# Gated linear attention and a gated feed-forward layer in one kernel: unit 0 through both ACT tables at once, loads reordered, decay and transposes moved

## Chip, cores and metric

The kernel runs on one core of a Trainium2 chip. The metric is the device time of one execution in microseconds (us). Engines: PE (matmul), PEld (its weight loads), DVE (VectorE), ACT (ScalarE), POOL (GpSimd, which here mostly issues the casting DMAs) and SP (SyncE, which issues the plain DMAs). "The trace" is the record of one profiled execution; its span is about 2 us shorter than the time.

## The reference, cut to what matters

```python
# attention: batch 4, 8 heads, 768 steps, head size 48; a decaying complex state per head
a_re, a_im = scaled so that |a| <= 0.999
for t in range(768):
    S_re, S_im = (a * S)_re + k[t] v[t]^T, (a * S)_im
    y[t] = q[t] @ S_re
# feed-forward on x = y as [3072 tokens, 384]
out = x + sigmoid(x @ w_res) * ((gelu(x @ w_gate) * (x @ w_val)) @ w_out)
```

The product of the decays over time is turned into cumulative sums of log-magnitude and angle. So each block of 256 steps needs Ln and Exp of `a` (one ACT table, a set of functions that ACT loads before it uses them, 1.28 us in these traces), then arctan and sin (another table); the feed-forward needs Gelu (a third).

## The kernel before

A group `g` is 256 steps of one batch (12 groups), a unit `u` is two groups (6 units). The program is software-pipelined. `phase_x(u)` does *gate math*: Ln/Exp for unit u+2 and u+1, arctan for u+2, sin for u+1, half of the attention of unit u, and the output matmuls (`op`) of unit u-1. `phase_y(u)` does the *gates*: `gp`, `vp`, `rp` of unit u, and the other half of an attention. A scheduler turns this program order into each engine's own order; in the timelines below an engine does not pass an instruction that waits. `E` and `Ei` are the exps of the cumulated log-magnitude and of its negative; `Q` and `K` are q and k multiplied by these and by the sines and cosines, made by DVE and then transposed by PE. "First Q" below is PE's first transpose of Q.

```python
    def p1_steps(g):
        ...  # lm = Ln(a_re); th = Exp(-lm) * a_im; s = Ln(1 + th^2); lm = min(lm + s/2, LNMAX)
    def decay(g):            # factor by which the state decays between groups: one [1,384] row of
                             # each of three tiles, turned to [96, 8] by way of DRAM
        md = dr.tile([3, DM], FP, tag="md", name="md")
        nc.gpsimd.dma_start(out=md[0:1, :], in_=T["E", g - 1][127:128, DM:W])
        nc.gpsimd.dma_start(out=md[1:2, :], in_=T["Ei", g][0:1, 0:DM])
        nc.gpsimd.dma_start(out=md[2:3, :], in_=T["lm", g][0:1, 0:DM])
        m3 = mp.tile([128, 3, H], FP, tag="m3", name="m3")
        for u in range(2):
            nc.gpsimd.dma_start(out=m3[u * D:(u + 1) * D]..., in_=md.rearrange("r (h d) -> d (r h)", h=H))
    def decay2(g):
        act(out=m3[0:DD, 2], in_=m3[0:DD, 2], func=AF.Exp)     # ACT waits for the DRAM round trip
        ...                                                    # M = product of the three, on DVE
    def xt_step(u, jj):      # x of one 128-token chunk, transposed for the feed-forward
        tpx = psT.tile([128, DM], BF, tag="tp", padded_shape=[128, 1024], name="tpx")
        ...
    def att_steps(u, half):
        steps = []
        for g in gs(u)[half:half + 1]:
            for c in range(C):
                steps += attention(g, c)
                steps.append(call(xt_step, u, half * C + c))
        return steps
    def phase_x(u):
        ...
        weave((0.0, 0.12, front), (0.05, 0.55, p1), (0.12, 0.45, exs), (0.46, 0.46, dec), (0.25, 0.65, cst),
              (0.69, 0.69, dec2), (0.7, 0.95, table_trig), (0.0, 0.8, att_steps(u, 1)), (0.1, 1.0, ops))
    ...
    for g in gs(0):
        load_a(g); load_q(g)               # (cut to one line each)
    for g in gs(1): load_a(g)
    for g in gs(1): load_q(g)
    for u in range(-2, NU + 1):            # two empty pipeline phases before unit 0's gates
        phase_x(u)
        if u == -2:
            load_w()                       # all weights, whole rows, no wait
        phase_y(u)
        ...
```

`weave` places lists of steps at fractions of a phase. `a`, `q`, `k` are loaded by SP; `v` and the weights are cast to bf16 while loading, by DMAs that POOL issues (the software queue).

Of the kernel before, what the change touches and what calls it, by code (L numbers as in the profile page):

```python
# [9 lines left out]
FP = mybir.dt.float32  # L10
BF = mybir.dt.bfloat16
AF = mybir.ActivationFunctionType
# [16 lines left out]
def kernel(  # L29
# [55 lines left out]
    wr = singles.tile([128, KD, DM], BF, name="wr")  # L85


    lda = ctx.enter_context(tc.tile_pool(name="lda", bufs=3))
    ldq = ctx.enter_context(tc.tile_pool(name="ldq", bufs=3))
    ldv = ctx.enter_context(tc.tile_pool(name="ldv", bufs=6))  # L90
    pA = ctx.enter_context(tc.tile_pool(name="pA", bufs=4))
    pS = ctx.enter_context(tc.tile_pool(name="pS", bufs=2))
    pE = ctx.enter_context(tc.tile_pool(name="pE", bufs=2))
    pQ = ctx.enter_context(tc.tile_pool(name="pQ", bufs=2))
# [24 lines left out]
    def act(**kw):  # L119
        tab(nc.scalar.activation(**kw))  # L120
# [22 lines left out]
            nc.gpsimd.dma_start(out=t[:, c], in_=rows(v, g, c))  # L143
        T["v", g] = t

    def load_w():
        for i in range(KD):
            nc.gpsimd.dma_start(out=wg[:, i, :], in_=moe_w_gate[i * 128:(i + 1) * 128, :])
            nc.gpsimd.dma_start(out=wv[:, i, :], in_=moe_w_val[i * 128:(i + 1) * 128, :])
        nc.gpsimd.dma_start(out=wr, in_=moe_w_res.rearrange("(i p) m -> p i m", p=128))  # L150
        for i in range(0, KF, 4):
            nc.gpsimd.dma_start(out=wo[:, i:i + 4, :],
                                in_=moe_w_out[i * 128:(i + 4) * 128, :].rearrange("(i p) m -> p i m", p=128))

    def flat(t):
        return t.rearrange("p c h d -> p (c h d)")


    def p1_steps(g):
        def s0():  # L160
            T["lm", g] = pA.tile([128, W], FP, tag="lm", name="lm")
            act(out=T["lm", g], in_=flat(T["ar", g]), func=AF.Ln)

        def s1():
            T["th", g] = pA.tile([128, W], FP, tag="th", name="th")
            act(out=T["th", g], in_=T["lm", g], func=AF.Exp, scale=-1.0)
            nc.vector.tensor_tensor(out=T["th", g], in0=T["th", g], in1=flat(T["ai", g]), op=OP.mult)  # L167

        def s2():
            T["s", g] = pS.tile([128, W], FP, tag="s", name="s")  # L170
            act(out=T["s", g], in_=T["th", g], func=AF.Square)

        def s3():
            act(out=T["s", g], in_=T["s", g], func=AF.Ln, bias=1.0)
            lm = T["lm", g]
            nc.vector.scalar_tensor_tensor(out=lm, in0=T["s", g], scalar=0.5, in1=lm, op0=OP.mult, op1=OP.add)
            nc.vector.tensor_scalar(out=lm, in0=lm, scalar1=LNMAX, scalar2=None, op0=OP.min)  # L177

        return [s0, s1, s2, s3]
# [5 lines left out]
    def cs_l(g, c):  # L185
# [9 lines left out]
            act(out=T["Ei", g][:, sl], in_=cs, func=AF.Exp, scale=-1.0)  # L195
        return ex

    def cs_t(g, c):
        s = g % NS
        th = T["th", g]  # L200
        if c == 0:
            T["fg", g] = pE.tile([128, C * H, 2, D], FP, tag="fg", name="fg")
            if s > 0:
                P = stt.tile([128, DM], FP, tag="P", name="P")
                nc.vector.tensor_tensor(out=P, in0=T["th", g - 1][:, DM:W], in1=th[:, 0:DM], op=OP.add)
                if s > 1:
                    nc.vector.tensor_tensor(out=P, in0=P, in1=T["P", g - 1], op=OP.add)
                T["P", g] = P
        sl = slice(c * DM, (c + 1) * DM)
        cs = psM.tile([128, DM], FP, tag="mm", padded_shape=[128, 512], name="cst")  # L210
        nc.tensor.matmul(out=cs, lhsT=tmat[c], rhs=th[:, sl], start=True, stop=(s == 0))
        if s > 0:
            nc.tensor.matmul(out=cs, lhsT=ones2pi, rhs=T["P", g], start=False, stop=True)
        cs3 = cs.rearrange("p (h d) -> p h d", h=H)
        fg = T["fg", g]
        hs = slice(c * H, (c + 1) * H)
        r = pS.tile([128, H, D], FP, tag="r", name="r")
        nc.vector.tensor_scalar(out=r, in0=cs3, scalar1=MAGIC, scalar2=MAGIC, op0=OP.add, op1=OP.subtract)
        nc.vector.tensor_tensor(out=fg[:, hs, 1, :], in0=cs3, in1=r, op=OP.subtract)
        nc.vector.scalar_tensor_tensor(out=fg[:, hs, 0, :], in0=fg[:, hs, 1, :], scalar=-1.0, in1=fg[:, hs, 1, :],  # L220
                                       op0=OP.mult, op1=OP.max)

    def p2_sin(g):
        T["CS", g] = pQ.tile([128, C * H, 2, D], BF, tag="CS", name="CS")
# [2 lines left out]
                             bias=hpi)  # L227
        act(out=T["CS", g][:, :, 1], in_=T["fg", g][:, :, 1], func=AF.Sin, scale=2.0 * math.pi)

    def decay(g):  # L230

        md = dr.tile([3, DM], FP, tag="md", name="md")
        nc.gpsimd.dma_start(out=md[0:1, :], in_=T["E", g - 1][127:128, DM:W])
        nc.gpsimd.dma_start(out=md[1:2, :], in_=T["Ei", g][0:1, 0:DM])
        nc.gpsimd.dma_start(out=md[2:3, :], in_=T["lm", g][0:1, 0:DM])
        m3 = mp.tile([128, 3, H], FP, tag="m3", name="m3")
        for u in range(2):
            nc.gpsimd.dma_start(out=m3[u * D:(u + 1) * D].rearrange("p r h -> p (r h)"),
                                in_=md.rearrange("r (h d) -> d (r h)", h=H))
        T["m3", g] = m3  # L240

    def decay2(g):
        m3 = T["m3", g]
        act(out=m3[0:DD, 2], in_=m3[0:DD, 2], func=AF.Exp)
        M = mp.tile([128, H], FP, tag="M", name="M")
        nc.vector.tensor_tensor(out=M[0:DD], in0=m3[0:DD, 0], in1=m3[0:DD, 1], op=OP.mult)
        nc.vector.tensor_tensor(out=M[0:DD], in0=M[0:DD], in1=m3[0:DD, 2], op=OP.mult)
        T["M", g] = M

    def products(g):  # L250
# [111 lines left out]
    def xt_step(u, jj):  # L362
        if jj == 0:
            T["xT", u] = xtp.tile([128, KD, 512], BF, tag="xT", name="xT")
        tpx = psT.tile([128, DM], BF, tag="tp", padded_shape=[128, 1024], name="tpx")
        x = T["x", u * 4 + jj]
        for f in range(KD):
            nc.tensor.transpose(out=tpx[:, f * 128:(f + 1) * 128], in_=x[:, f * 128:(f + 1) * 128], identity=ident)  # L368
        dst = T["xT", u][:, :, jj * 128:(jj + 1) * 128]
        src = tpx.rearrange("p (f t) -> p f t", f=KD)  # L370
        if jj % 2 == 0:
            nc.scalar.copy(out=dst, in_=src)
        else:
            nc.vector.tensor_copy(out=dst, in_=src)  # L374
# [41 lines left out]
    def table(nm):  # L416
        def f():
            tab(nc.scalar.preload_act_table_set(nm))  # L418
        return f

    def gs(u):
        return [2 * u, 2 * u + 1] if 0 <= u < NU else []

    def call(f, *a):
        return lambda: f(*a)

    def zip_steps(lists):
        return [st for tup in zip(*lists) for st in tup]

    def att_steps(u, half):  # L430

        steps = []
        for g in gs(u)[half:half + 1]:
            for c in range(C):
                steps += attention(g, c)
                steps.append(call(xt_step, u, half * C + c))
        return steps

    def phase_x(u):

        pend = []

        def csl(g, c):
            pend.append(cs_l(g, c))

        def ex():
            pend.pop(0)()
        front = [call(csl, g, c) for g in gs(u + 1) for c in range(C)]
        p1 = zip_steps([p1_steps(g) for g in gs(u + 2)])
        exs = [ex for _ in gs(u + 1) for _ in range(C)]  # L450
        dec = [call(decay, g) for g in gs(u + 1) if g % NS > 0]
        cst = [call(cs_t, g, c) for g in gs(u + 1) for c in range(C)]
        dec2 = [call(decay2, g) for g in gs(u + 1) if g % NS > 0]
        trig = [table("trig_and_small")] + [call(p1_arctan, g) for g in gs(u + 2)] + [call(p2_sin, g) for g in gs(u + 1)]
        ops = [call(op_step, u - 1, jj) for jj in range(4)] if 0 <= u - 1 < NU else []
        if p1 or exs:
            table("natural_log_exp_and_others")()
            table_trig = trig
        else:
            table_trig = []  # L460
        weave((0.0, 0.12, front), (0.05, 0.55, p1), (0.12, 0.45, exs), (0.46, 0.46, dec), (0.25, 0.65, cst),
              (0.69, 0.69, dec2), (0.7, 0.95, table_trig), (0.0, 0.8, att_steps(u, 1)), (0.1, 1.0, ops))

    def phase_y(u):

# [5 lines left out]
        pr = [st for g in gs(u + 1) for st in products(g)]  # L471
        weave((0.0, 1.0, gv), (0.0, 0.4, pr), (0.3, 0.95, att_steps(u + 1, 0)))

    for g in gs(0):
        load_a(g)
        load_q(g)
    for g in gs(1):
        load_a(g)
    for g in gs(1):
        load_q(g)  # L480
    for u in range(-2, NU + 1):
        phase_x(u)
        if u == -2:
            load_w()
        phase_y(u)
        for g in gs(u + 4):
            load_a(g)
        if u >= -1:
            for g in gs(u + 3):
                load_q(g)  # L490


# [28 lines left out]
```

## Time and profile before

| | before |
|---|---|
| time, median of 3 runs | 384.78 us |
| profiled span | 380.7 us |
| first Q transpose / first gate matmul (`gp`) | 75.1 / 116.9 us |
| end of the gates of unit 0 | 139.0 us |
| PE idle from first `gp` to the end (263.8 us) | 26.9 us |

The page of the kernel before, busy tenths in 40 slices of 9.5 us each; PEclk is the granted PE clock in tenths.

```profile
PE   0000077284559998669989799886999899998995
DVE  1000429487887449939859798589975899654434
ACT  2000774687354579084596845994557455552440
PEclk9999998669558999969999899998999999998999
DMA  9999999999944048930466552051000210001002
```

In the first four slices little but DMA works; until slice 12 PE is mostly far from full. (PEclk is not to be trusted in the first slices: two `csl` matmuls at 47.5 us, recorded at 1.00, took 1.65 us, as long as two of the same size at 71.1 us, recorded at 0.50 (1.62 us); two at 63.2 us, recorded at 1.00, took 0.88 us.) Later, PE is rarely below 8 except in a few slices. These lie where gate math runs. The table of windows shows it (columns: start and end, length, busy time of PE, PEld, DVE, ACT, POOL with instruction counts, granted clock, DMA share, GB/s); the first line is the ramp, then the gates of unit 0, the gate math before unit 1's gates, those gates, and the next gate math.

```profile
0.00:116.87 116.87, 41.41 (x260) 26.42 (x262) 56.05 (x102) 52.18 (x78) 30.18 (x49) 0.83 1.18 154
116.87:139.02 22.15, 21.99 (x167) 12.12 (x170) 13.13 (x23) 11.96 (x22) 1.52 (x2) 0.98 0.11 6
139.02:169.18 30.16, 21.95 (x152) 13.06 (x150) 19.44 (x39) 21.21 (x35) 7.43 (x11) 0.89 0.83 113
169.18:192.71 23.53, 23.15 (x192) 13.26 (x195) 21.28 (x37) 12.28 (x23) 1.80 (x2) 1.00 0.21 44
192.71:217.05 24.34, 20.60 (x156) 12.45 (x154) 18.35 (x36) 20.64 (x34) 6.56 (x8) 0.93 0.67 90
```

PE is idle 8.2 us of the first gate-math stretch. The timeline of ACT there (start, length, instruction, and in brackets the idle time before it and what ended it) shows why:

```profile
152.09 0.59 ACT L295 COPY qk<-tp 96x512 bf16<-96x512 bf16 x1
156.92 0.21 ACT L120 ACTIVATE m_1258<-m_1258 96x8 f32<-96x8 f32 x1 [4.24 <-DMA m_1258<-md]
161.67 0.21 ACT L120 ACTIVATE m_1265<-m_1265 96x8 f32<-96x8 f32 x1 [4.54 <-DMA m_1265<-md]
161.90 1.28 ACT L418 ACT_TABLE_LOAD   x1
163.19 1.57 ACT L120 ACTIVATE th<-th 128x768 f32<-128x768 f32 x2
164.67 0.46 ACT L343 CAST x<-y 128x384 bf16<-128x384 f32 x1
```

Two 0.2 us instructions on [96, 8] hold ACT for 8.8 us, since each waits for a row that goes to DRAM and back. The copy of `x` (164.67) stands behind them, although PE had finished its input `y` by 155.4 us. PE waits for that copy with its transpose `tpx` and runs nothing else meanwhile, from its own timeline:

```profile
165.19 0.50 PE L368 MATMUL tpx<-ident,x 128*128 128x128 bf16 x3 [7.05 <-ACT x L343]
```

### The profile page before, as it was taken

To read this page: it belongs to the slowest core of one execution; us is meant where nothing else is said; L and a number is where in the kernel's file an instruction comes from. 1 tells how busy PE (TensorE), PEld (TensorE's weight loads), DVE (VectorE), ACT (ScalarE), POOL (GpSimd) and SP (SyncE) were. 2 spreads that over 40 slices of the span, in tenths; PEclk is the share of its full clock that TensorE was granted. 3 is DMA by queue.
4 is the path that set the end of the run, shared out by engine and by line. 5 is a ranking of instruction groups with operands and counts; after the bars stand their busy time and mean duration, and the time that the engine had idled before them with its cause. 6 is when DMAs were issued, how large, how long until landed. Compare 5 with 4: busy or idle time off the path is not lost.

```text
span 380.7 us, 5497 instructions
## 1 busy us (share of the span) xinstructions
PE 278.4 (73%) x2059; PEld 162.7 (43%) x2080; DVE 247.6 (65%) x452; ACT 205.6 (54%) x340; POOL 56.0 (15%) x84
## 2 busy tenths in 40 slices
PE   0000077284559998669989799886999899998995
PEld 0000033163445565335556355553555565564453
DVE  1000429487887449939859798589975899654434
ACT  2000774687354579084596845994557455552440
POOL 9330043011201013400022300021001400000000
PEclk9999998669558999969999899998999999998999
DMA  9999999999944048930466552051000210001002
GB/s 134 149 206 187 183 171 174 142 136 162 149 79 28 2 21 164 138 34 22 84 63 108 61 107 41 2 104 43 21 3 3 23 43 21 2 22 62 2 1 83
DMA packets 132667, 30.25 MB, mean 79 GB/s; under 512 B 126881, under 2 KB 131873, under 8 KB 132641
## 3 DMA queue, kind: packets, MB, share of 16 engines
q1 hardware_dynamic: 103296, 23.60, 35.8%
q0 software_dynamic: 29344, 6.31, 18.7%
q8 instruction: 16, 0.26, 0.3%
q14 instruction: 11, 0.08, 0.1%
HBM read 31.33 MB, written 4.76 MB: 95 GB/s over the span
## 4 chain that ended last, share of the span: by engine, by line
PE 35%; DVE 7%; ACT 6%; issue 5%; DMA 5%; POOL 1%; POOLq 0%; ACTq 0%; DVEq 0%
PE gp L383 10%; PE vp L387 10%; PE op L407 5%; PE rp L399 3%; ACT L418 2%; DMA md<-Ei 1%; PE tp L290 1%; PE at L300 1%; PE tp L293 1%; ACT th L120 1%; PE dk L330 1%; PE y L338 1%; DMA m_3114<-md 1%; DVE ot L410 1%; DMA m_2530<-md 1%
## 5 line engine op out<-in xcount | busy, mean ns | idle before, releaser
L383 PE MATMUL gp<-xT,wg 128*128 128x512 bf16 x203 | 60.7, 388 | 5.0 <-DVE xT L374 3.8
L387 PE MATMUL vp<-xT,wv 128*128 128x512 bf16 x208 | 60.9, 387 | 0.2
L191 PE MATMUL csl<-lm,lt0a 128*128 128x384 f32 x24 | 11.4, 562 | 49.7 <-DVE lm L177 49.7
L167 DVE TENSOR_TENSOR th<-th,ai 128x768 f32<-128x768 f32 x12 | 11.4, 953 | 45.4 <-DMA ai<-in_a_im_dram 38.2
L295 ACT COPY qk<-tp 96x512 bf16<-96x512 bf16 x48 | 27.9, 582 | 20.7 <-PE tp L293 18.7
L303 DVE TENSOR_TENSOR atm<-at,mask_81 128x512 bf16<-128x512 f32 x48 | 32.9, 686 | 9.0 <-PE at L300 8.7
L143 POOL DMA_DIRECT2D v<-in_v_dram x24 | 22.0, 932 | 71.2 <-PE y L340 71.2
L383 PEld LDWEIGHTS <-wg 128*128 128x128 bf16 x216 | 20.4, 99 | 23.2 <-issue 6.0
L120 ACT ACTIVATE lm<-ar 128x768 f32<-128x768 f32 x12 | 9.7, 838 | 38.0 <-DMA ar<-in_a_re_dram 38.0
L296 DVE COPY qk<-tp 96x512 bf16<-96x512 bf16 x48 | 19.9, 415 | 14.8 <-ACT qk L295 14.5
L387 PEld LDWEIGHTS <-wv 128*128 128x128 bf16 x216 | 20.5, 100 | 20.7 <-issue 2.9
L290 PE MATMUL tp<-ident,Q 128*96 128x128 bf16 x192 | 20.3, 233 | 11.6 <-DVE qk L296 6.6
L290 PEld LDWEIGHTS <-Q 128*96 128x96 bf16 x192 | 18.0, 133 | 23.9 <-issue 12.4
L191 PEld LDWEIGHTS csl<-lm,lt0a 128*128 128x128 f32 x24 | 4.7, 212 | 52.8 <-DVE lm L177 47.5
L418 ACT ACT_TABLE_LOAD x20 | 25.7, 1283 | 1.1 <-PEq L505 0.7
L338 PEld LDWEIGHTS <-atm 128*128 128x128 bf16 x192 | 12.3, 98 | 24.6 <-DVE atm L303 23.7
L338 PE MATMUL y<-v,atm 128*128 128x48 bf16 x192 | 16.6, 189 | 8.5 <-DVE atm L303 8.4
L293 PE MATMUL tp<-ident,K 128*96 128x128 bf16 x192 | 21.2, 234 | 0.0
L410 DVE SCALAR_TENSOR_TENSOR ot<-sg,op 128x384 f32<-128x384 f32 x24 | 13.1, 546 | 11.7 <-PE op L407 11.7
L300 PE MATMUL at<-qk 96*128 96x128 bf16 x192 | 20.0, 230 | 0.7 <-DVE qk L296 0.6
L343 ACT CAST x<-y 128x384 bf16<-128x384 f32 x24 | 11.4, 477 | 13.3 <-PE y L340 11.5
L368 PE MATMUL tpx<-ident,x 128*128 128x128 bf16 x72 | 9.1, 235 | 12.0 <-ACT x L343 12.0
(124 smaller groups left out, 636.8 us busy)
## 6 DMA issues: line engine op xcount, KB each, us to landing
ar<-in_a_re_dram SPq DMA_DIRECT2D x24, 192.0 KB, 4.5
ai<-in_a_im_dram SPq DMA_DIRECT2D x24, 192.0 KB, 5.1
q<-in_q_dram SPq DMA_DIRECT2D x24, 192.0 KB, 4.4
k<-in_k_dram SPq DMA_DIRECT2D x24, 192.0 KB, 4.2
out_dram<-ot SPq DMA_DIRECT2D x24, 192.0 KB, 1.9
v<-in_v_dram POOLq DMA_DIRECT2D x24, 96.0 KB, 5.3
wg<-in_moe_w_gate_dram POOLq DMA_DIRECT2D x3, 384.0 KB, 15.0
wv<-in_moe_w_val_dram POOLq DMA_DIRECT2D x3, 384.0 KB, 15.0
```

The source lines that it names most:

```text
L143: nc.gpsimd.dma_start(out=t[:, c], in_=rows(v, g, c))
L290: nc.tensor.transpose(out=tp[0:DD, j * 128:j * 128 + 128], in_=Q(x), identity=ident)
L293: nc.tensor.transpose(out=tp[0:DD, 512 + j * 128:640 + j * 128], in_=K(x), identity=ident)
L295: nc.scalar.copy(out=qk[0:DD, 0:512], in_=tp[0:DD, 0:512])
L296: nc.vector.tensor_copy(out=qk[0:DD, 512:1024], in_=tp[0:DD, 512:1024])
L300: nc.tensor.matmul(out=at[:, j], lhsT=qk[0:DD, 512 + j * 128:640 + j * 128], rhs=qk[0:DD, j * 128:j * 128 + 128], start=True, stop=True)
L303: nc.vector.tensor_tensor(out=atm, in0=at, in1=mask4, op=OP.mult)
L338: nc.tensor.matmul(out=ys, lhsT=st["atm", hg][:, j], rhs=V(h), start=True, stop=first)
L383: nc.tensor.matmul(out=gp, lhsT=wg[:, fi, ffi * 128:(ffi + 1) * 128], rhs=xT[:, fi, :], start=(fi == 0), stop=(fi == KD - 1))
L387: nc.tensor.matmul(out=vp, lhsT=wv[:, fi, ffi * 128:(ffi + 1) * 128], rhs=xT[:, fi, :], start=(fi == 0), stop=(fi == KD - 1))
L407: nc.tensor.matmul(out=ps, lhsT=h2[:, ffi, jj * 128:(jj + 1) * 128], rhs=wo[:, ffi, :], start=(ffi == 0), stop=(ffi == KF - 1))
L418: tab(nc.scalar.preload_act_table_set(nm))
```

## The change

Its intent: fill the pipeline in fewer steps and take waits out of ACT's and PE's order. Unit 0's Ln/Exp and arctan/sin run in one phase before the first; `a` of four groups is loaded first; the weights of the gates come in column quarters and only after the first `k` has landed, `w_out` after the first `k` of unit 1; the log row of the decay is turned a phase earlier, so that ACT's small exp finds it ready, and the product with the E and Ei rows is left to DVE at the end; `tpx` gets a buffer of the large PSUM pool and comes one step later; `lm` and `th` overwrite their inputs, which pays for more load buffers.

```diff
-    lda = ctx.enter_context(tc.tile_pool(name="lda", bufs=3))
-    ldq = ctx.enter_context(tc.tile_pool(name="ldq", bufs=3))
+    lda = ctx.enter_context(tc.tile_pool(name="lda", bufs=6))
+    ldq = ctx.enter_context(tc.tile_pool(name="ldq", bufs=4))
-    pA = ctx.enter_context(tc.tile_pool(name="pA", bufs=4))
 ...
+    def load_w_in():
+        FQ = FF // 4
+        for i in range(4):
+            for w, src in ((wg, moe_w_gate), (wv, moe_w_val)):
+                nc.gpsimd.dma_start(out=w[:, :, i * FQ:(i + 1) * FQ],
+                                    in_=src[:, i * FQ:(i + 1) * FQ].rearrange("(i p) m -> p i m", p=128))
 ...
+    def after_landing(t, f):
+        w = singles.tile([1, 1], FP, name="landed%d" % len(T))
+        i = nc.gpsimd.tensor_copy(out=w, in_=t[0:1, C - 1, H - 1, D - 1:D])
+        with tc.issue_after(i.ins):
+            f()
 ...
+    def decay0(g):
+        turn("m1", g, [T["lm", g][0:1, 0:DM]])          # DRAM round trip, one phase early
+    def decay1(g):
+        act(out=m[0:DD], in_=m[0:DD], func=AF.Exp)      # m = T["m1", g]
     def decay2(g):
+        turn("m2", g, [T["E", g - 1][127:128, DM:W], T["Ei", g][0:1, 0:DM]])
+    def decay3(g):                                      # M = m2[0] * m2[1] * m1, on DVE
 ...
-        tpx = psT.tile([128, DM], BF, tag="tp", padded_shape=[128, 1024], name="tpx")
+        tpx = psM.tile([128, DM], BF, tag="mm", padded_shape=[128, 1024], name="tpx")
 ...
-                steps.append(call(xt_step, u, half * C + c))
+                if c > 0:
+                    steps.insert(-1, call(xt_step, u, half * C + c - 1))
+            steps.append(call(xt_step, u, half * C + C - 1))
 ...
+        if u < 0:
+            for f in [st for g in g1 for st in p1(g)] + csls + exs + dec + zip_steps([p1(g) for g in g2]) + dec1:
+                f()
+            for f in atn[:1] + [call(p1_arctan, g) for g in g1] + cst + sin + atn[1:] + dec3:
+                f()
+            return
+        weave((0.0, 0.12, csls), (0.05, 0.5, zip_steps([p1(g) for g in g2])), (0.01, 0.01, dec1), (0.12, 0.45, exs),
+              (0.46, 0.46, dec), (0.2, 0.65, cst), (0.7, 0.95, atn + sin), (0.95, 0.95, dec3), (0.0, 0.8, att), (0.1, 1.0, ops))
 ...
+    for g in gs(0) + gs(1):
+        load_a(g)
     for g in gs(0):
-        load_a(g)
         load_q(g)
 ...
+    after_landing(T["k", 0], load_w_in)
+    for u in range(-1, NU + 1):
 ...
+        if u == -1:
+            for g in gs(1):
+                load_q(g)
+            after_landing(T["k", 2], load_w_out)
```

More of the change, by code (lines that the diff above doesn't have):

```diff
@@ L144, in load_q, with load_w_out @@
         T["v", g] = t
-    def load_w():
-        for i in range(KD):
-            nc.gpsimd.dma_start(out=wg[:, i, :], in_=moe_w_gate[i * 128:(i + 1) * 128, :])
-            nc.gpsimd.dma_start(out=wv[:, i, :], in_=moe_w_val[i * 128:(i + 1) * 128, :])
+    def load_w_in():
[4 more added lines that the diff above has]
+                                    in_=src[:, i * FQ:(i + 1) * FQ].rearrange("(i p) m -> p i m", p=128))
         nc.gpsimd.dma_start(out=wr, in_=moe_w_res.rearrange("(i p) m -> p i m", p=128))
+    def load_w_out():
         for i in range(0, KF, 4):
@@ L160, in s0 @@
         def s0():
-            T["lm", g] = pA.tile([128, W], FP, tag="lm", name="lm")
-            act(out=T["lm", g], in_=flat(T["ar", g]), func=AF.Ln)
+            T["lm", g] = flat(T["ar", g])
+            T["th", g] = flat(T["ai", g])
+            act(out=T["lm", g], in_=T["lm", g], func=AF.Ln)
         def s1():
-            T["th", g] = pA.tile([128, W], FP, tag="th", name="th")
-            act(out=T["th", g], in_=T["lm", g], func=AF.Exp, scale=-1.0)
-            nc.vector.tensor_tensor(out=T["th", g], in0=T["th", g], in1=flat(T["ai", g]), op=OP.mult)
+            T["s", g] = pS.tile([128, W], FP, tag="s", name="s")
+            act(out=T["s", g], in_=T["lm", g], func=AF.Exp, scale=-1.0)
+            nc.vector.tensor_tensor(out=T["th", g], in0=T["s", g], in1=T["th", g], op=OP.mult)
         def s2():
-            T["s", g] = pS.tile([128, W], FP, tag="s", name="s")
             act(out=T["s", g], in_=T["th", g], func=AF.Square)
@@ L196, in cs_l, with carry @@
         return ex
+    def carry(g):
+        s = g % NS
+        if s > 0:
+            P = stt.tile([128, DM], FP, tag="P", name="P")
+            nc.vector.tensor_tensor(out=P, in0=T["th", g - 1][:, DM:W], in1=T["th", g][:, 0:DM], op=OP.add)
+            if s > 1:
+                nc.vector.tensor_tensor(out=P, in0=P, in1=T["P", g - 1], op=OP.add)
+            T["P", g] = P
     def cs_t(g, c):
@@ L202, in cs_t @@
             T["fg", g] = pE.tile([128, C * H, 2, D], FP, tag="fg", name="fg")
-            if s > 0:
-                P = stt.tile([128, DM], FP, tag="P", name="P")
-                nc.vector.tensor_tensor(out=P, in0=T["th", g - 1][:, DM:W], in1=th[:, 0:DM], op=OP.add)
-                if s > 1:
-                    nc.vector.tensor_tensor(out=P, in0=P, in1=T["P", g - 1], op=OP.add)
-                T["P", g] = P
         sl = slice(c * DM, (c + 1) * DM)
@@ L219, in cs_t @@
         nc.vector.tensor_tensor(out=fg[:, hs, 1, :], in0=cs3, in1=r, op=OP.subtract)
-        nc.vector.scalar_tensor_tensor(out=fg[:, hs, 0, :], in0=fg[:, hs, 1, :], scalar=-1.0, in1=fg[:, hs, 1, :],
-                                       op0=OP.mult, op1=OP.max)
+        if c == C - 1:
+            nc.vector.scalar_tensor_tensor(out=fg[:, :, 0, :], in0=fg[:, :, 1, :], scalar=-1.0, in1=fg[:, :, 1, :],
+                                           op0=OP.mult, op1=OP.max)
     def p2_sin(g):
@@ L228, in p2_sin, with turn @@
         act(out=T["CS", g][:, :, 1], in_=T["fg", g][:, :, 1], func=AF.Sin, scale=2.0 * math.pi)
-    def decay(g):
-        md = dr.tile([3, DM], FP, tag="md", name="md")
-        nc.gpsimd.dma_start(out=md[0:1, :], in_=T["E", g - 1][127:128, DM:W])
-        nc.gpsimd.dma_start(out=md[1:2, :], in_=T["Ei", g][0:1, 0:DM])
-        nc.gpsimd.dma_start(out=md[2:3, :], in_=T["lm", g][0:1, 0:DM])
-        m3 = mp.tile([128, 3, H], FP, tag="m3", name="m3")
+    def turn(nm, g, srcs):
+        n = len(srcs)
+        md = dr.tile([n, DM], FP, tag="d" + nm, name="d" + nm)
+        for i, src in enumerate(srcs):
+            nc.gpsimd.dma_start(out=md[i:i + 1, :], in_=src)
+        m = mp.tile([128, n, H], FP, tag=nm, name=nm)
         for u in range(2):
-            nc.gpsimd.dma_start(out=m3[u * D:(u + 1) * D].rearrange("p r h -> p (r h)"),
+            nc.gpsimd.dma_start(out=m[u * D:(u + 1) * D].rearrange("p r h -> p (r h)"),
                                 in_=md.rearrange("r (h d) -> d (r h)", h=H))
-        T["m3", g] = m3
+        T[nm, g] = m
+    def decay0(g):
+        turn("m1", g, [T["lm", g][0:1, 0:DM]])
+    def decay1(g):
+        m = T["m1", g]
+        act(out=m[0:DD], in_=m[0:DD], func=AF.Exp)
     def decay2(g):
-        m3 = T["m3", g]
-        act(out=m3[0:DD, 2], in_=m3[0:DD, 2], func=AF.Exp)
+        turn("m2", g, [T["E", g - 1][127:128, DM:W], T["Ei", g][0:1, 0:DM]])
+    def decay3(g):
+        m = T["m2", g]
         M = mp.tile([128, H], FP, tag="M", name="M")
-        nc.vector.tensor_tensor(out=M[0:DD], in0=m3[0:DD, 0], in1=m3[0:DD, 1], op=OP.mult)
-        nc.vector.tensor_tensor(out=M[0:DD], in0=M[0:DD], in1=m3[0:DD, 2], op=OP.mult)
+        nc.vector.tensor_tensor(out=M[0:DD], in0=m[0:DD, 0], in1=m[0:DD, 1], op=OP.mult)
+        nc.vector.tensor_tensor(out=M[0:DD], in0=M[0:DD], in1=T["m1", g][0:DD, 0], op=OP.mult)
         T["M", g] = M
@@ L427, in zip_steps @@
     def zip_steps(lists):
-        return [st for tup in zip(*lists) for st in tup]
+        return [st[i] for i in range(max(map(len, lists), default=0)) for st in lists if i < len(st)]
     def att_steps(u, half):
@@ L441, in phase_x @@
         pend = []
+        g1, g2 = gs(u + 1), gs(u + 2)
+        d1 = [g for g in g1 if g % NS > 0]
+        d2 = [g for g in g2 if g % NS > 0]
+        ops = [call(op_step, u - 1, jj) for jj in range(4)] if 0 <= u - 1 < NU else []
+        att = att_steps(u, 1)
+        if not g1:
+            weave((0.0, 0.8, att), (0.1, 1.0, ops))
+            return
         def csl(g, c):
@@ L447, in ex, with p1 @@
             pend.pop(0)()
-        front = [call(csl, g, c) for g in gs(u + 1) for c in range(C)]
-        p1 = zip_steps([p1_steps(g) for g in gs(u + 2)])
-        exs = [ex for _ in gs(u + 1) for _ in range(C)]
-        dec = [call(decay, g) for g in gs(u + 1) if g % NS > 0]
-        cst = [call(cs_t, g, c) for g in gs(u + 1) for c in range(C)]
-        dec2 = [call(decay2, g) for g in gs(u + 1) if g % NS > 0]
-        trig = [table("trig_and_small")] + [call(p1_arctan, g) for g in gs(u + 2)] + [call(p2_sin, g) for g in gs(u + 1)]
-        ops = [call(op_step, u - 1, jj) for jj in range(4)] if 0 <= u - 1 < NU else []
-        if p1 or exs:
-            table("natural_log_exp_and_others")()
-            table_trig = trig
-        else:
-            table_trig = []
-        weave((0.0, 0.12, front), (0.05, 0.55, p1), (0.12, 0.45, exs), (0.46, 0.46, dec), (0.25, 0.65, cst),
-              (0.69, 0.69, dec2), (0.7, 0.95, table_trig), (0.0, 0.8, att_steps(u, 1)), (0.1, 1.0, ops))
+        def p1(g):
+            return p1_steps(g) + ([call(decay0, g)] if g % NS > 0 else [])
+        csls = [call(csl, g, c) for g in g1 for c in range(C)]
+        exs = [ex for _ in g1 for _ in range(C)]
+        dec = [call(decay2, g) for g in d1]
+        atn = [table("trig_and_small")] + [call(p1_arctan, g) for g in g2]
+        cst = [call(carry, g) for g in g1] + [call(cs_t, g, c) for g in g1 for c in range(C)]
+        sin = [call(p2_sin, g) for g in g1]
+        dec1 = [call(decay1, g) for g in d1]
+        dec3 = [call(decay3, g) for g in d1]
+        table("natural_log_exp_and_others")()
+        if u < 0:
[3 more added lines that the diff above has]
+                f()
+            return
+        weave((0.0, 0.12, csls), (0.05, 0.5, zip_steps([p1(g) for g in g2])), (0.01, 0.01, dec1), (0.12, 0.45, exs),
+              (0.46, 0.46, dec), (0.2, 0.65, cst), (0.7, 0.95, atn + sin), (0.95, 0.95, dec3), (0.0, 0.8, att), (0.1, 1.0, ops))
     def phase_y(u):
@@ L472, in phase_y @@
         weave((0.0, 1.0, gv), (0.0, 0.4, pr), (0.3, 0.95, att_steps(u + 1, 0)))
+    for g in gs(0) + gs(1):
+        load_a(g)
     for g in gs(0):
-        load_a(g)
         load_q(g)
-    for g in gs(1):
-        load_a(g)
-    for g in gs(1):
-        load_q(g)
-    for u in range(-2, NU + 1):
-        phase_x(u)
-        if u == -2:
-            load_w()
-        phase_y(u)
-        for g in gs(u + 4):
-            load_a(g)
-        if u >= -1:
-            for g in gs(u + 3):
-                load_q(g)
+    after_landing(T["k", 0], load_w_in)
+    for u in range(-1, NU + 1):
+        phase_x(u)
+        for g in gs(u + 3):
+            load_a(g)
+        if u == -1:
+            for g in gs(1):
+                load_q(g)
+            after_landing(T["k", 2], load_w_out)
+        phase_y(u)
+        for g in gs(u + 3):
+            load_q(g)
 _INS = ['q', 'k', 'v', 'a_re', 'a_im', 'moe_w_gate', 'moe_w_val', 'moe_w_out', 'moe_w_res']
```

## The prediction

> What bounds the kernel now. Two stretches, by the timeline and the table of windows. (1) The ramp: the first matmul starts at 47.5 us, the first gate matmul (gp) at 116.9 us. In 0 to 40 us the compute engines are nearly empty (ACT 3.7 us busy, PE none) while DMA is full. All weights (3.8 MB as landed) sit on the software queue from 9 us; the second group's a_re, issued at 11 us, landed only at 38 us (25 us, against a median of 4.5). The Trainium skill, "DMA: Bandwidth & Descriptors", section "Queues, rings and completion order", says that each DMA engine takes queues in turn, packet by packet; this delay agrees. From the first Q at 74.1 us, DVE is about 80% busy until 117 us, at a PE clock near 0.5 to 0.6. (2) From 116.9 us to the end, 264 us, PE is busy 237 us: 27 us idle, some 4 of it at the end. The idle time lies in the stretches with gate math (33.7, 24.0, 29.1, 22.0 us long, PE idle 8.4, 3.7, 5.9, 1.7 us). The chain and the waits of ACT show why: the small exp for the decay waits in ACT's order on a DRAM round trip (ACT idle 4.2+4.5, 3.4, 1.5+1.2 us), so table load, arctan and sin come late, then gelu, then the gates.
>
> What the change does. Compute work hardly changes: the |f| operation is done once per group of 256 rows instead of twice (saves under 2 us of DVE). It moves:
> - Ramp: a of four groups first, then q/k of unit 0; weights only after the first k. Unit 0's Ln/Exp and Arctan/Sin now run without passing through a whole extra phase. At the measured 140 to 170 GB/s shared with twelve v loads, a of groups 0 and 1 lands by about 19 us, all of a by 33, q/k of group 0 by 37. Then table load, arctan, cst, fg, sin: first Q at about 47 us instead of 74.
> - New cost: weights (from about 37 us, 16 to 22 us of transfer) now compete with q/k of group 1 and a of unit 2. Group 2's single-row decay transfer is behind all weights on the software queue, and its exp stands in ACT's order just after the next table load, before most of the first attention: I expect ACT to stop there until about 62 us. After it some 22 us of DVE work remain before the gates, with latencies 28 to 32 us. First gp at about 93 us: 24 us earlier.
> - Steady: the lm decay factor is taken a phase earlier and the E/Ei product is made on DVE after the sins, so ACT no longer waits on DRAM; tpx leaves the tp buffer and comes a step later (PE waited 12.0 us on x for tpx, 7.1 once). Ceiling 22 us of PE idle; I count 12.
>
> Sum: 384.8 - 24 - 12 = 349 us. Range 336 to 365.
>
> What would show it: first gp at 88 to 98 us; first Q 44 to 52; PE idle from first gp to end about 15 us instead of 27; no ACT wait on m over 1 us in later units, but one ACT wait of 5 us or more on m near 55 to 63 us in the ramp; gate-math stretches of 22 to 27 us; PE, DVE, ACT busy sums unchanged within 3%.
>
> What would make it wrong: weights, issued later in 1.5 KB pieces, starve a of unit 2 beyond 75 us (then gp after 100 and about 360 us); the decay wait is short because packets interleave (then 338); psM, now also holding tpx, stalls gp/vp; DVE, 80% busy in the gate stretches, becomes their limit and the steady gain vanishes (about 360).
>
> Chances: faster 0.94, same 0.05, slower 0.01.

## The result and the profile after

The median is 343.26 us (342.10 to 344.25, 4 runs) against 383.82 us for the kernel before in the same rounds. The ratio is 0.895, 95% interval 0.889 to 0.901.

The page of the changed kernel, slices of 8.5 us:

```profile
PE   0330544298689979899897999779999989999995
DVE  1322696249999649999389998499994799855443
ACT  3365434349665696756896656977568275662530
PEclk9996585559699999999999999999999999999999
DMA  9999999999999999527422620021000210002002
```

PE is at 7 to 9 from slice 11 on until the last slice, at full clock. The same windows as before (ramp, gates of unit 0, gate math, gates of unit 1, gate math):

```profile
0.00:89.85 89.85, 36.65 (x236) 23.75 (x237) 46.64 (x82) 46.81 (x72) 35.21 (x57) 0.75 1.33 165
89.85:119.45 29.60, 27.79 (x262) 17.20 (x268) 26.36 (x47) 17.87 (x32) 6.13 (x9) 0.94 1.31 166
119.45:139.39 19.94, 16.46 (x79) 9.26 (x78) 14.81 (x26) 16.24 (x27) 6.38 (x10) 1.00 1.00 160
139.39:166.60 27.21, 26.49 (x270) 16.45 (x275) 25.35 (x49) 17.35 (x31) 2.52 (x4) 1.00 0.35 50
166.60:185.83 19.23, 15.26 (x75) 8.49 (x74) 14.04 (x25) 16.07 (x27) 6.32 (x10) 1.00 0.42 58
```

The gate-math stretches are 5 to 10 us shorter, but look at the counts. PE executes 79 instructions there where it executed 152, and 270 instead of 192 in the gates. The attention has moved out of the gate math into the gates. So a stretch by itself tells little; the sums do. From the traces: the time to the first `gp` fell by 27.0 us; the five gate-math stretches fell from 116.4 to 85.1 us in sum; the six gate stretches rose from 135.6 to 154.7; the last output stretch is 11.8 in both. That gives -27.0 - 31.3 + 19.1 = -39.2 us of the 39.3 by which the span fell. A cut at the end of unit 0's gates gives 139.0 to 119.4 (19.6 us), and from there to the end 241.7 to 222.0 (19.7 us). Neither cut has equal work before it. By the PE instructions in the traces, at the first `gp` the changed kernel has run 236 where the kernel before had run 260, and at the end of unit 0's gates 498 where it had run 427. So for the later part 12.3 us (from the first `gp`) is too low and 19.7 us too high a measure of the gain; experiment 6 has a kernel with the old order of work, which measures it better.

ACT in the first gate-math stretch, which answers to the timeline shown before:

```profile
120.00 1.28 ACT L445 ACT_TABLE_LOAD   x1
121.29 0.21 ACT L119 ACTIVATE m_641<-m_641 96x8 f32<-96x8 f32 x1
121.41 0.19 ACT L119 ACTIVATE m_678<-m_678 96x8 f32<-96x8 f32 x1
121.51 1.56 ACT L119 ACTIVATE ar<-ar 128x768 f32<-128x768 f32 x2
...
130.48 1.28 ACT L445 ACT_TABLE_LOAD   x1
131.78 1.58 ACT L119 ACTIVATE ai<-ai 128x768 f32<-128x768 f32 x2
133.66 0.48 ACT L399 COPY xT<-tpx 128x384 bf16<-128x384 bf16 x1 [0.31 <-PE tpx L395]
```

The two small exps have no wait. The second table load comes 10.5 us after the first, where it came 22.3 us after it in the kernel before (139.57 to 161.90).

In the ramp one long ACT wait is left, on the same kind of instruction. The timelines of ACT and of POOL:

```profile
54.14 1.28 ACT L445 ACT_TABLE_LOAD   x1
64.32 0.21 ACT L119 ACTIVATE m_268<-m_268 96x8 f32<-96x8 f32 x1 [8.90 <-DMA m_268<-dm_266]
64.44 0.83 ACT L119 ACTIVATE ar<-ar 128x768 f32<-128x768 f32 x1
```

```profile
42.82 0.76 POOL L152 DMA_DIRECT2D wr<-in_moe_w_res_dram  x1
44.80 0.54 POOL L253 DMA_DIRECT2D dm_266<-ar  x1 [1.23 <-DVE fg L235]
58.97 1.29 POOL L256 DMA_DIRECT2D m_268<-dm_266  x2 [13.62 <-DMA dm_266<-ar]
```

A row of 1.5 KB issued at 44.8 us, just behind nine weight loads, took until 59 us to land. The Trainium skill ("DMA: Bandwidth & Descriptors", section "SWDGE vs HWDGE vs iDMA") says that only one queue of the software kind is allocated, so such a row shares its queue with the weights; this trace agrees: its list of DMA queues has one software queue, q0. Experiments 1, 8 and 9 test whether bulk loads in front delay such a row.

### The profile page after: what moved, and what is told of

It is laid out like the page before. It is cut to its first block, busy times and chain, and to the rows that moved or that the text cites. A ratio compares the mean times of both kernels' runs of the same rounds, so it can differ in the third digit from the quotient of the medians.

```text
span 341.4 us, 5552 instructions
## 1 busy us (share of the span) xinstructions
PE 267.3 (78%) x2054; PEld 160.6 (47%) x2080; DVE 245.4 (72%) x440; ACT 203.0 (59%) x338; POOL 67.1 (20%) x104
## 4 chain that ended last, share of the span: by engine, by line
PE 47%; DMA 18%; DVE 15%; ACT 9%; issue 7%; POOL 3%; ACTq 0%; DVEq 0%; POOLq 0%
PE vp L414 12%; PE gp L410 11%; PE op L434 6%; DMA dm_266<-ar 4%; DMA v<-in_v_dram 4%; PE tp L320 3%; PE at L327 3%; PE tp L317 3%; PE rp L426 3%; DMA dm_663<-Ei 2%; ACT L445 2%; DVE fg L237 2%; DVE r L234 2%; DMA dm_219<-ar 2%; ACT CS L119 2%
## 5 line engine op out<-in xcount | busy, mean ns | idle before, releaser
L410 PE MATMUL gp<-xT,wg 128*128 128x512 bf16 x196 | 61.5, 382 | 7.6 <-DVE xT L401 4.6
L322 ACT COPY qk<-tp 96x512 bf16<-96x512 bf16 x48 | 27.9, 581 | 28.3 <-PE tp L320 15.1
L180 DVE TENSOR_TENSOR ai<-s,ai 128x768 f32<-128x768 f32 x12 | 11.1, 955 | 38.5 <-ACT s L119 26.9
L142 POOL DMA_DIRECT2D v<-in_v_dram x24 | 21.3, 902 | 43.0 <-PE y L367 22.4
L323 DVE COPY qk<-tp 96x512 bf16<-96x512 bf16 x48 | 19.9, 414 | 10.1 <-ACT qk L322 9.6
L203 PE MATMUL csl<-ar,lt0a 128*128 128x384 f32 x24 | 12.3, 601 | 18.6 <-DVE ar L189 18.5
L119 ACT ACTIVATE CS<-fg,hpi 128x768 bf16<-128x768 f32 x12 | 11.2, 935 | 24.1 <-DVE fg L237 24.1
L445 ACT ACT_TABLE_LOAD x18 | 23.1, 1283 | 1.0 <-PEq L547 0.7
L320 PE MATMUL tp<-ident,K 128*96 128x128 bf16 x192 | 22.1, 235 | 0.0
L227 PE MATMUL cst<-ai,lt0b 128*128 128x384 f32 x24 | 11.6, 568 | 13.4 <-ACT ai L119 13.1
L365 PE MATMUL y<-v,atm 128*128 128x48 bf16 x192 | 17.9, 187 | 2.5 <-DVE atm L330 2.4
L365 PEld LDWEIGHTS <-atm 128*128 128x128 bf16 x192 | 13.5, 98 | 12.8 <-DVE atm L330 11.6
L320 PEld LDWEIGHTS <-K 128*96 128x96 bf16 x192 | 17.3, 133 | 0.0
L357 PEld LDWEIGHTS <-K 128*96 128x96 bf16 x160 | 13.3, 138 | 6.5 <-DVE K L292 4.2
## 6 DMA issues: line engine op xcount, KB each, us to landing
wv<-in_moe_w_val_dram POOLq DMA_DIRECT2D x4, 288.0 KB, 10.5
```

The source lines that it names most:

```text
L142: nc.gpsimd.dma_start(out=t[:, c], in_=rows(v, g, c))
L320: nc.tensor.transpose(out=tp[0:DD, 512 + j * 128:640 + j * 128], in_=K(x), identity=ident)
L322: nc.scalar.copy(out=qk[0:DD, 0:512], in_=tp[0:DD, 0:512])
L323: nc.vector.tensor_copy(out=qk[0:DD, 512:1024], in_=tp[0:DD, 512:1024])
L365: nc.tensor.matmul(out=ys, lhsT=st["atm", hg][:, j], rhs=V(h), start=True, stop=first)
L410: nc.tensor.matmul(out=gp, lhsT=wg[:, fi, ffi * 128:(ffi + 1) * 128], rhs=xT[:, fi, :], start=(fi == 0), stop=(fi == KD - 1))
```

## The experiments

All kernels gave correct results. Labels that begin with `a` are edits of the changed kernel, `b` of the kernel before. Each ran beside the kernel before on the same chip. As a rule one part of the change is undone; a loss is then what that part is worth in the presence of the others. The changed kernel is at 0.895 (0.889 to 0.901) and 343.3 us. It ran in other rounds than the experiments; the medians of the kernel before lie between 382.4 and 384.8 us over the rounds, so differences of 2 or 3 us whose intervals overlap are not clear of noise.

### 1. Weights early again (a_w_early)

```diff
-    after_landing(T["k", 0], load_w_in)           # column quarters
+    load_w_in(); load_w_out()                     # whole rows, at once
```

> The changed kernel with only the weight loads put back: whole rows, all issued at once behind the first v loads, no wait for the first k. Theory A (in the ramp the gain comes from keeping the weights away from the first a loads): group 1's a lands some 15 to 20 us later, first Q at 62 us or later instead of 47, time 355 to 362 us (changed kernel 343). Rival B (the ramp gain comes from running unit 0 through both tables without a whole extra phase): time 343 to 348, first Q before 53 us.

Measured: 345.45 us, ratio 0.904 (0.899 to 0.909), which is not clear of the changed kernel's. Half of theory A came true and had little effect: the first Q came 12.7 us later (60.9 us; 62 or more was expected), but the first `gp` only 1.7 us later (91.5). The ACT timeline shows two opposite effects: Ln of group 1 now waits 12.8 us for its `a`, and the 8.9 us wait on the small decay row at 64 us is gone. With no weights in front, the row's first transfer takes at most 4.0 us instead of 13.9; ACT also comes to the small exp later, at 67.8 us. So holding the weights back mostly moved a wait from before the first Q to after it.

### 2. Weights late in the kernel before (b_w_late)

```diff
-            load_w()
+            after_landing(T["k", 0], load_w)
```

> The kernel before with only the weights held back until the first k has landed. Theory A (weights starve the first a loads): group 1's a_re lands before 20 us instead of 38, first Q at 50 to 58 us instead of 74, time 362 to 370 us (before 384). Rival B (the order of tables is what counts in the ramp): 378 to 385 us.

Measured: 380.62 us, ratio 0.996 (0.993 to 1.000). Theory A's time and first Q were missed here too. `a_re` of group 1 did land by 20.5 us instead of 38.4, as the ACT timeline says, but the first Q came at 73.7 us:

```profile
20.50 0.84 ACT L120 ACTIVATE lm<-ar 128x768 f32<-128x768 f32 x1 [15.19 <-DMA ar<-in_a_re_dram]
36.08 0.84 ACT L120 ACTIVATE s<-th 128x768 f32<-128x768 f32 x1 [12.13 <-DVE th L173]
49.93 0.84 ACT L120 ACTIVATE lm<-ar 128x768 f32<-128x768 f32 x1 [7.36 <-DMA ar<-in_a_re_dram]
54.00 0.84 ACT L120 ACTIVATE lm<-ar 128x768 f32<-128x768 f32 x1 [3.22 <-DMA ar<-in_a_re_dram]
68.02 0.21 ACT L120 ACTIVATE m<-m 96x8 f32<-96x8 f32 x1 [5.75 <-DMA m<-md]
```

This is not a clean test of theory A. The first `k` released the weights at 17.2 us, when `a_im` of group 1 was just being issued (15.1 to 19.5 us); it then took up to 17.7 us to land, and ACT waited 12.1 us for the product with it (36.08). So the wait moved from `a_re` to `a_im`. In this table order unit 0's sin stands behind unit 1's Ln and Exp, and `a` of unit 1 was issued only from 40.4 us on, as SP's issues of `q` and `k` before it took from 19.5 to 40.4 us while the weights landed. The small decay exp waits once more at 68 us.

### 3. Unit 0's tables as before (a_phases_old)

```diff
-        if u < 0:                                  # unit 0 through both tables
-            ...
+    (phases from u = -2 again, loads unchanged)
```

> The changed kernel with unit 0 going through the tables as before (a phase for unit 0's Ln/Exp and arctan, then one for unit 1's Ln/Exp and unit 0's sin), loads unchanged. Theory A (load order made the ramp gain): 343 to 347 us, as sin of unit 0 still waits for unit 1's Ln/Exp in both. Rival B (table order): 350 us or more, first Q later than 53 us.

Measured: 350.52 us, ratio 0.917 (0.915 to 0.918): rival B on time. Yet the first Q (48.9 us) was not later. The loss is after it: the first `gp` comes at 96.7 us instead of 89.9, and the rest of the program from the end of unit 0's gates is unchanged (222.1 us against 222.0). ACT waits 22.3 us on small decay rows in two places, 13.1 us in the longer. The table order therefore pays 7 us, in the second half of the ramp.

### 4. Weights in whole rows, still late (a_w_rows)

```diff
-        for i in range(4): ... w[:, :, i * FQ:(i + 1) * FQ]
+        for i in range(KD): ... w[:, i, :]
```

> The changed kernel with weights in whole rows instead of column quarters, still held until the first k. All weights land by about 58 us and the first gate matmul comes at 90, so quarters should be worth nothing: 342 to 345 us. If the larger pieces take more of the DMA engines from q/k of group 1 and a of unit 2: up to 348, with ACT waiting on a after the small exp.

Measured: 343.92 us, ratio 0.900 (0.895 to 0.905). No difference from quarters is shown. The weights of the gates have landed by about 55 us, long before the first `gp` at 87.9 us.

### 5. The decay as before (a_decay_old)

```diff
-        decay0 / decay1 / decay2 / decay3
+        decay  (three rows in one round trip)  /  decay2  (exp on ACT at 0.69, then DVE)
```

> The changed kernel with only the decay put back: one DRAM round trip for all three rows and the small exp behind it in ACT's order ahead of arctan and sin. Theory A (the 12 us of the steady part come from ACT no longer waiting on DRAM): 352 to 356 us, with ACT waits of 3 to 9 us on m3 in each gate-math stretch but the last. Rival B (they come from the moved tpx): 342 to 346 us. If both count for half: 348.

Measured: 358.88 us, ratio 0.940 (0.934 to 0.946), more than theory A asked for. 15.6 us are lost: 7.2 by the end of unit 0's gates, 7.8 after it (span 356.4, gates of unit 0 end at 126.7). The waits of ACT over the whole span agree with theory A's cause (waiting instruction, releaser, total us, times, longest):

```profile
ACT m L119 <- DMA m<-dm: 32.7, 8, 12.2
```

After the first `gp` they are 18.8 us in six waits, the longest 7.0; in two of the four later stretches they are 2.8 and 1.4 us, below the 3 to 9 expected. In the changed kernel the only such line is the 8.9 us in the ramp.

### 6. tpx as before (a_tpx_old), and only its buffer as before (a_tpx_buf_old)

```diff
# a_tpx_old: both hunks; a_tpx_buf_old: the first only
-        tpx = psM.tile([128, DM], BF, tag="mm", ...)
+        tpx = psT.tile([128, DM], BF, tag="tp", ...)
-                if c > 0:
-                    steps.insert(-1, call(xt_step, u, half * C + c - 1))
-            steps.append(call(xt_step, u, half * C + C - 1))
+                steps.append(call(xt_step, u, half * C + c))
```

> The changed kernel with only tpx put back: in the tp buffer, right after its own chunk. Theory A (the decay made the steady gain): 343 to 346 us, although the attention goes back into the gate-math stretches (those about 5 us longer, the gate stretches about 5 us shorter). Rival B (tpx made it): 351 to 356 us, with PE waiting about 10 us on x for tpx as before.

Measured: 354.37 us, ratio 0.927 (0.923 to 0.931): rival B. 11.1 us for a move that adds and removes no instruction. The first `gp` comes at 100.9 us instead of 89.9. PE's timeline in the ramp shows the stop:

```profile
66.61 0.29 PE L395 MATMUL tpx<-ident,x 128*128 128x128 bf16 x1 [11.47 <-ACT x L370]
```

PE stood at `tpx` for 11.5 us, and `x` stood in ACT's order behind the small exp that was waiting for its row. After unit 0's gates PE waits only 0.6 us on `x`. The other kernel tells the buffer from the order:

> The changed kernel with tpx back in the single tp buffer, but still one step later than its own chunk. Both put back cost 11.1 us. Theory A (the buffer: tpx of a chunk and the tp of the next chunk take turns in one buffer, so attention is held to the pace of ACT and DVE copies): 350 to 355 us. Rival B (the order: PE reaching tpx before ACT has made x): 343 to 346 us.

Measured: 340.76 us, ratio 0.888 (0.879 to 0.897): rival B, the order, though below its range. With the old buffer the attention went back into the gate-math stretches (the gates of unit 1 take 23.8 us, as before the change), and nothing was lost. So the large move of attention between stretches is a side effect of the buffer that has no use for the time. Whether the old buffer is even a little better isn't settled; its interval overlaps that of the changed kernel. The two kernels with the old buffer have the same order of work as the kernel before (427 PE instructions up to the end of unit 0's gates in all three). Compared with each other, the order costs 8.0 us up to there (123.9 and 115.8 us) and 5.2 us after it (228.7 and 223.5). The 11.5 us wait on `x` agrees with the loss in the ramp; how the order costs 5.2 us later is not shown.

### 7. Decay and tpx both as before (a_decay_tpx_old)

> The changed kernel with both the decay and tpx put back; undone alone they cost 15.6 and 11.1 us. Theory A (two separate stalls): 366 to 371 us. Rival B (both only move where the one backlog of DVE and PE work waits, so they overlap): 358 to 363 us, little more than the decay alone.

Measured: 372.41 us, ratio 0.971 (0.965 to 0.976): theory A, and slightly above its range. Both undone cost 29.1 us, a little more than 15.6 + 11.1. From the end of unit 0's gates to the end this kernel takes 243.9 us, against 241.7 in the kernel before (equal work) and 222.0 in the changed one. All of the steady gain is thus in these two parts. The first Q still comes at 48.0 us, but the first `gp` only at 104.4. What is left to the loads, the table order, the buffers and the in-place tiles is the distance from 372.4 to the kernel before, 10.8 us, all of it in the ramp.

### 8. The small exp later (a_dec1_late)

```diff
-  (0.01, 0.01, dec1),
+  (0.52, 0.52, dec1),       # end of the Ln/Exp work of the phase
```

> The changed kernel with the small exp of the lm row put at the end of the Ln/Exp work of its stretch instead of at its start. In the changed kernel ACT stops 8.9 us on it, to 64.3 us, in the ramp. Theory A (this wait is on the chain): 335 to 338 us, first gate matmul at 82 to 85 us instead of 89.9. Rival B (q/k of group 1 and a of unit 2, slowed by the weights, would bind there anyway, or DVE's backlog): 340 to 343 us, the wait turning into one on DMA a or k.

Measured: 345.45 us, ratio 0.902 (0.895 to 0.909). Neither theory: the first `gp` did come at 84.8 us, 5.1 us earlier, and then the gates of unit 0 took 38.0 us instead of 29.6. DVE's timeline:

```profile
84.53 0.54 DVE L235 TENSOR_TENSOR fg<-cst,r 128x384 f32<-128x384 f32 x1
91.76 0.16 DVE L273 TENSOR_TENSOR M<-m 96x8 f32<-96x8 f32 x1 [6.68 <-DMA m<-dm]
```

The wait had moved to the next small row, that of E and Ei. (In time the run is not clear of the changed kernel.) POOL's timeline shows the same picture as for the first, with `w_out` in front:

```profile
68.51 2.27 POOL L156 DMA_DIRECT2D wo<-in_moe_w_out_dram  x3
70.75 1.79 POOL L142 DMA_DIRECT2D v<-in_v_dram  x2
72.49 0.56 POOL L253 DMA_DIRECT2D dm<-Ei  x1
85.50 1.48 POOL L256 DMA_DIRECT2D m<-dm  x2 [12.45 <-DMA dm<-Ei]
```

This suggested the next kernel.

### 9. The same, and w_out behind that row (a_dec1_wo)

```diff
-            after_landing(T["k", 2], load_w_out)
+        if u == 0:
+            i = nc.gpsimd.tensor_copy(out=w, in_=T["m2", 2][0:1, 0, 0:1])   # the row has landed
+            with tc.issue_after(i.ins):
+                load_w_out()
```

> The small exp at the end of its stretch as in the earlier run (which removed ACT's 8.9 us wait but gained nothing: DVE then waited 6.7 us on the E/Ei decay row, whose transfer sat 12.5 us behind w_out on the software queue), and w_out now issued only after that row has landed. Theory A (what binds is small decay transfers behind bulk loads on the one software queue): DVE's wait on m for group 2 below 2 us, unit 0's gates end at 112 to 116 us instead of 119.5, time 336 to 340. Rival B (the loads of a and q/k for units 1 and 2 bind in any case): 342 to 345.

Measured: 337.56 us, ratio 0.881 (0.878 to 0.884): theory A in every number. The same row, issued at nearly the same time:

```profile
72.07 0.53 POOL L253 DMA_DIRECT2D dm<-Ei  x1 [2.77 <-ACT Ei L119]
76.10 1.48 POOL L256 DMA_DIRECT2D m<-dm  x2 [3.50 <-DMA dm<-Ei]
```

3.5 us of waiting instead of 12.5. DVE has no wait on this row among its larger ones, and the gates of unit 0 end at 115.6 us. The next rows, issued at 84.6 us with `w_out` now in front of them, waited 10.7 us. So bulk loads in front of a row cause its delay. Whether they do so through the one software queue or through the DMA engines that all queues share is not separated: `k` loads that SP issued on its own queue in the same stretch (66 to 84 us) also landed later with `w_out` there, in a median of 8.3 us (experiment 8) against 5.5.

### 10. v of units 1 and 2 later (a_v_late), and all three together (a_v_dec1_wo)

In the changed kernel POOL issues twelve `v` loads in the first 13 us, eight of them for units that come much later.

```diff
+        if g in gs(0) or g > 5:
+            load_v(g)
 ...
-            after_landing(T["k", 2], load_w_out)
+            def vs():
+                for g in gs(1) + gs(2): load_v(g)
+                load_w_out()                    # in a_v_late only
+            after_landing(T["k", 0], vs)
```

> The changed kernel with the eight v loads of units 1 and 2 held until the first k has landed; twelve v loads shared the first 25 us with a. If the ramp is bound by the a and q/k loads up to first Q: all a 3 to 5 us earlier, first Q at 43 to 44 us, time 338 to 340. If the wait on the small decay transfer behind the weights binds instead, which starts after the first k: it also moves forward with k, minus what eight v loads cost later; 339 to 343. A worse time than 345 would say that the delayed v loads hit the attention of unit 1.

Measured: 338.40 us, ratio 0.885 (0.883 to 0.887), as expected: first Q at 43.7 us, gates of unit 0 end at 114.3 instead of 119.4, the rest as before. The edit moves `w_out` too: it is issued from 56.3 us, behind the `v` loads, instead of 68.5, so the gain is not that of the `v` loads alone.

> The same with the eight v loads of units 1 and 2 held until the first k, which alone gave 338.4 us. Theory A: both gains add, 331 to 335 us. Rival B (total bytes of the ramp bind): 336 to 339, with ACT waiting on a.

Measured: 331.30 us, ratio 0.866 (0.862 to 0.870). Theory A: both gains add (5.7 and 4.9 us alone, 12.0 together). Here `w_out` waits for the small row as in experiment 9, so against that kernel only the `v` loads differ: they are worth 6.3 us. This version beats both kernels; by the two ratios it is 3% faster than the changed one. The first Q is at 40.9 us, the first `gp` at 75.7, and the gates of unit 0 end at 105.0.

## Why the prediction was right, and which of its steps were not

The time (343.3 us) lies in the range of 336 to 365, 6 us below the forecast of 349. Point by point:

1. *The marks in the profile held in the ramp.* First Q: forecast 47 us, DVE made it at 47.2 and PE took it at 48.2. First `gp`: forecast 93 (88 to 98), measured 89.9. One ACT wait on a small row near 55 to 63 us: measured 8.9 us, ending at 64.3. That the weights ahead of the row delay it is shown by experiment 1, and for the next row and `w_out` by the pair of kernels 8 and 9; that it is the software queue, and not the DMA engines, is not shown.
2. *The share of the parts was wrong in the ramp.* The prediction gave 24 us to the new order of loads and tables. With the decay and `tpx` as before (experiment 7) this order still brings the first Q to 48.0 us, but the first `gp` only to 104.4: 12.5 of the 27.0 us. The other 14.5 came from the decay and from `tpx`, which the prediction counted for the later units only. Undone alone, the weights' late start is worth 2.2 us (not clear of noise) and the table order 7.3. So the step that failed is the credit of 24 us to loads and tables, which measured 12.5. The reading behind it, "the second group's a_re, issued at 11 us, landed only at 38 us", is true, but no run shows that this held the ramp: when it landed by 20.5 us (experiment 2), the kernel gained under 2 us, as `a_im` of the same group was late in its place; when it was late in the changed kernel (experiment 1), the first `gp` came only 1.7 us later.
3. *The steady gain was mis-sized.* The forecast was 12 us after the first `gp`. Measured from the first `gp` it is 12.3, but that is in part luck: in the changed kernel 24 fewer PE instructions come before this point, so more are left after it. At equal work, by the kernel with the old buffer (experiment 6), 23.2 us are gained up to the end of unit 0's gates and 18.2 after it. Of the 18.2, the decay gives 15.2 and the order of `tpx` 5.2, and the rest costs 2.2 (241.7, 243.9, 228.7 and 223.5 us: kernel before, experiment 7, the two of experiment 6). Of the 23.2 the rest gives 10.8, the decay 4.4 and the order 8.0. In another sequence the shares may differ.
4. *Gate-math stretches of 22 to 27 us:* measured 18.1 to 19.9 in four of them and 8.0 in the last, since attention left them; the forecast did not see this, and it turned out not to matter (experiment 6).
5. *PE idle about 15 us:* measured 20.9 of 251.6 us, so this mark was missed. PE's busy time in that part also fell, from 237.0 to 230.7 us, at a clock of 0.99 instead of 0.97. So half of the 12.3 us is idle time and half shorter busy time. The Trainium skill ("TensorE: Matmul & The Clock Gate", section "What's actually happening") says that PE drops to half clock after an idle window of about 3.4 us; the trace of the kernel before agrees in the stretch with the 7 us `tpx` wait: PE stopped at 158.1 us, the recorded clock fell from 1.00 to 0.50 at about 162.2, and it was back at 1.00 at about 169.0, 3.8 us after PE had begun again.
6. *No ACT wait on a decay row above 1 us in later units:* held. *Busy sums within 3%:* DVE 247.6 to 245.4 and ACT 205.6 to 203.0 hold; PE 278.4 to 267.3 is 4%, so this mark was missed.

Left open: the in-place tiles, the larger load pools and the merged absolute value of `f` were not tried alone. The four parts undone singly add up to 36.2 us of a gap of 40. That leaves little for the three, but it does not measure them: parts undone singly need not add up (two of them together cost 29.1 us, not 26.7).

## What to carry to other kernels

Look at the smallest instructions that wait for a DMA round trip in an engine's fixed order: what they cost is everything that stands behind them, here also a PE that waits for a copy on that engine. Move such an instruction behind its data, and issue bulk loads after the transfer that it needs (putting that transfer on another queue was not tried). When a whole load order is changed, ask whether the bytes that must land before the steady part get fewer; the loads that were merely swapped here moved a wait (experiments 1 and 2), while loads that are not needed yet (the `v` of later units) could be moved away for a real gain (experiment 10).

## What the Trainium skill lacked or had wrong

- "DMA: Bandwidth & Descriptors", section "Anatomy of one DMA": its fit for one software DMA is about 2.0 us plus a term for the size. A row of 1.5 KB held its successor for 3.5 us with two `v` loads in front and the same row 12.5 us with `w_out` in front as well; another such row behind nine weight loads 13.6 us. I found no warning there about small transfers issued behind bulk loads.
- "ScalarE: Activation LUTs", section "What ACT_TABLE_LOAD costs": the load of 1283 ns is as measured here, but the drain of about 1380 ns that it adds for each switch does not appear: in the changed kernel the load at 130.48 us follows an instruction that ended at 130.47, and the next one starts at 131.78, so the switch took 1.3 us.
- "TensorE: Matmul & The Clock Gate", section "What's actually happening": full clock after about 3.4 us of sustained work. In the ramp of the changed kernel PE began again at 66.2 us, had one gap of 0.8 us (70.2 to 71.0) among its recorded matmuls, and was granted 0.50 until about 76.0 us: 9.8 us after the start and 5.0 after the gap. The page does not say how much of a window may be idle.
